# A list-scheduled attention and expert kernel: transfers planned at 260 GB/s, joins of w_outT in place, a table of whole rows, another order of the last accumulators

## The chip, the cores and the metric

The kernel runs on one core of a Trainium2 chip. The metric is the device time of one execution in microseconds (us). Engines are called TensorE (PE), VectorE (DVE), ScalarE (ACT), GpSimd (POOL) and SyncE (SP); SP issues nearly all transfers, GpSimd those with indices. TensorE's weight loads stand in the profile as an engine of their own, PEld.

## The reference

Three steps follow one another, all in float32 but for two matrices of the second:

```python
scores = scale * np.matmul(q, k.transpose(0, 1, 3, 2)) - np.log(S)   # 4 batches, 12 heads, 448 tokens, 64
x = np.matmul(1.0 / (1.0 + np.exp(-scores)), v)                      # then 1792 tokens x 768
h = x @ w_in                                                        # 768 -> 2048
x = np.where(h > 0, h, np.exp(np.minimum(h, 0)) - 1) @ w_out         # 2048 -> 768
logits = x @ w_gate                                                 # 8 experts
for idx in np.argsort(-logits.flatten()):                           # best pairs first, 224 tokens an expert
    ...
out[mask] = np.maximum(x[mask] @ w1[e], 0) @ w2[e]                   # for each expert: 768 -> 1024 -> 768
```

w_in and w_out are float64 and reach the chip as pairs of 32-bit words.

## The kernel before

**Arithmetic.** A float32 factor is split into a high part in TensorE's faster format (`hcopy`, on ScalarE or VectorE) and the rest (`lsub`, always VectorE). A product takes three matmuls: high by high, high by rest, rest by high.

**Stages.** `attention(b)` works through 24 units of two heads for each of 4 batches; its scores go through ScalarE's sigmoid. `layer1(b)` has 16 pieces `f` of 128 columns of w_in, each of 18 matmuls of 128x448 into one of a ring of accumulator banks; a piece is evacuated by two ScalarE functions and two VectorE SCALAR_TENSOR_TENSOR, then split. The second of these VectorE instructions (`zone<-zone,bank 128x448` in the rows) is the last that reads the bank. `layer2(b)` has 6 rows `d` of 48 matmuls over two pieces of w_out. Layer 1 of a batch is interleaved with the attention of the next.

**Joins.** For batch 0 a piece of w_in (768 KB as float64) or w_out (1 MB) is loaded into one of two arena buffers, and `join` (L450) makes float32 of it: ScalarE copies the upper words scaled (ACTIVATE), VectorE masks and shifts them (TENSOR_SCALAR), takes in the sign and then the lower words (two SCALAR_TENSOR_TENSOR). There are 16 + 12 such pieces. The joined piece is written to a DRAM copy, from which later batches load it; each is then split by `hcopy` and `lsub` in `weights` (L495).

**The product of w_out and w_gate.** `through(k)` (L462), six times in layer 1 of batches 1 and 2, before pieces 3, 8 and 13, loads a block of w_outT as two halves of 1 MB, joins each through a slot of the weight ring, and multiplies them by w_gate. It gives the router's logits of the last batch early.

**Rows.** `rows_out` (L663) transposes each 128 columns of x and writes them to two DRAM tables of 512 and 256 columns. For each of 8 experts (phases) VectorE searches the threshold, `listing` (L886) makes the list of tokens, and GpSimd gathers the rows by index: two tables by two groups of 112 tokens, four instructions a phase. `gathered` transposes them on TensorE; `expert` (L970) runs the two layers, with expert weights that stream in as 64 pieces of 768 KB, and scatters rows to the output.

**What sets the order.** All instructions are recorded first. `Plan.run` (L133) then simulates the engines and writes out each engine's queue: at each step the instruction that can start first, and of those within 0.02 us the one with the lowest priority number. That number is the order of creation less a boost (`plan.first(n)`). Its costs are formulas; a transfer ends after its bytes at an assumed rate plus constants. On the chip each engine then executes its queue strictly in that order, so the formulas decide who stands ahead of whom, and the chip's own durations decide who waits. The lines are:

```python
dma = max(dma, s + 1.1) + op.lat      # L195, in Plan.run
op.end = dma + 1.0
lat=n * size / 360e3                  # L279, in Plan.dma, and in fetch (L949)
```

Almost every row of the profile has line L247, where recorded instructions are issued; operations are told apart by their tiles: `zone`, `zone_r` (work tiles), `arena` (raw words), `bank` and `twin` (accumulators, a twin being two banks).

Of the kernel before, what the change touches and what calls it, by code (L numbers as in the profile page):

```python
# [52 lines left out]
class Plan:  # L53
# [79 lines left out]
    def run(self):  # L133
        clock = {e: 0.0 for e in self.eng}
        dma = 0.0
# [26 lines left out]
        while n < len(self.ops):  # L162
# [31 lines left out]
            if e == "SP":  # L194
                dma = max(dma, s + 1.1) + op.lat  # L195
                op.end = dma + 1.0
# [76 lines left out]
    def dma(self, out, in_):  # L273
        size = mybir.dt.size(out.dtype)
        n = 1
        for d in out.shape:
            n *= d
        self.add([("SP", 0.06, lambda: self.eng["SP"].dma_start(out, in_))], [self.region(in_)], [self.region(out)],
                 lat=n * size / 360e3)  # L279

# [10 lines left out]
def kernel(  # L291
# [43 lines left out]
    DA = 4 * P  # L335
    x2rows = [dram.tile([NT, n], F32, name=f"x2rows{i}") for i, n in enumerate((DA, DM - DA))]

# [124 lines left out]
    def through(k):  # L462
# [3 lines left out]
        for hf in range(2):  # L466
            x = r_raw()
            if wide:
                plan.dma(x, w_outT[k, hf])
                y = x.rearrange("p a b -> p (a b)")[:, :KH * P].rearrange("p (a b) -> p a b", b=P).bitcast(F32)  # L470
                join(y, x, r_wd())
            else:
                y = x.rearrange("p a b -> p (a b)")[:, :KH * P].rearrange("p (a b) -> p a b", b=P).bitcast(F32)
                plan.dma(y, w_outT[k, hf])
            ws.append(y.rearrange("p a b -> p (a b)"))
# [100 lines left out]
    def layer1(b):  # L576
        ws = {}
        for f in range(-2, KF):
# [3 lines left out]
            if f < 0:  # L582
                continue
            if b in (1, 2) and f in (3, 8, 13):
                through((b - 1) * 3 + f // 5)
# [77 lines left out]
    def rows_out(b, d, x2, e):  # L663
        rows, pr = r_rows(), sc()[:, 0] if b < B - 1 else twins[0][:, 0]
        with plan.unit():
            for c in range(C):
                PE.transpose(pr[:CP, c * P:(c + 1) * P], x2[:, c * CP:(c + 1) * CP], ident)
        e.copy(rows, pr[:CP, :C * P].rearrange("p (c x) -> p c x", c=C))
        x, o = x2rows[d // 4], d % 4 * P
        plan.dma(x[b * S:(b + 1) * S, o:o + P].rearrange("(c p) x -> p c x", p=CP), rows)  # L670

# [210 lines left out]
    def indirect(reads, writes, lat=GL, **kw):  # L882
        plan.add([("G", 1.05, lambda: plan.eng["G"].indirect_dma_start(**kw))], [plan.region(x) for x in reads],  # L883
                 [plan.region(x) for x in writes], lat=lat)

    def listing(ph):  # L886
# [27 lines left out]
        xg = [r_xg() for _ in range(NA)]  # L914
        for i, c in enumerate((slice(0, DA), slice(DA, DM))):
            for a in range(NA):
                indirect([x2rows[i], idx], [xg[a][:, c]], GL if ph else GL0, out=xg[a][:, c], out_offset=None,
                         in_=x2rows[i], in_offset=bass.IndirectOffsetOnAxis(ap=idx[:, a:a + 1], axis=0))
# [30 lines left out]
    def fetch(g):  # L949
# [7 lines left out]

        plan.add([("SP", 0.06, go)], [(f"reg{ph}", 0, 1, 0, 1)], [plan.region(x)], lat=P * WB * 4 / 360e3)
        h, l = r_eh(), r_el()
# [10 lines left out]
    def expert(ph):  # L970
# [31 lines left out]
        idx = lists.pop(ph)[0]  # L1002
        for a in range(NA):
            y = r_y()
            for n in range(2):
                if ph == E - 1:
                    for f in range(NB):
                        layer(ys, hH, hL, *ws[f // 2], f, f % 2, [2 * a + n])
                AV_.copy(y[:, n * DH:(n + 1) * DH], ys[2 * a + n][:CP, :DH])
            indirect([idx, y], [], out=out, out_offset=bass.IndirectOffsetOnAxis(ap=idx[:, a:a + 1], axis=0),  # L1010
                     in_=y, in_offset=None)

# [80 lines left out]
```

## Time and profile before

| | us |
|---|---|
| median of 3 runs | 1019.3 |
| the three runs | 1016.2, 1019.3, 1023.8 |
| the profiled execution | 1016.5 |
| its span | 1014.7 |
| TensorE busy | 974.2 (96%) |
| VectorE busy | 743.0 (73%) |
| ScalarE busy | 458.1 (45%) |
| GpSimd busy | 60.5 (6%) |
| transfers on SP's queue | 160.48 MB |

The profile is of one execution. Views cut it in different ways: shares of the whole span, shares of chosen stretches (with the granted TensorE clock as a fraction of full speed), groups of like instructions with count and mean duration, sums of waits by what ended them, and the instructions of an engine in order of time. A bracket such as `[2.40 <-DVE zone L247]` says how long the engine stood idle before the row and what ended that. The share of the whole span is an average over stages with different limits, so stretches and single waits tell more.

### The profile page before, as it was taken

To read this page: it belongs to the slowest core of one execution; us is meant where nothing else is said; L and a number is where in the kernel's file an instruction comes from. 1 tells how busy PE (TensorE), PEld (TensorE's weight loads), DVE (VectorE), ACT (ScalarE), POOL (GpSimd) and SP (SyncE) were. 2 spreads that over 40 slices of the span, in tenths; PEclk is the share of its full clock that TensorE was granted. 3 is DMA by queue.
4 is the path that set the end of the run, shared out by engine and by line. 5 is a ranking of instruction groups with operands and counts; after the bars stand their busy time and mean duration, and the time that the engine had idled before them with its cause. 6 is when DMAs were issued, how large, how long until landed. Compare 5 with 4: busy or idle time off the path is not lost. (4 is left out here: it accounts for less than half of the span.)

```text
span 1014.7 us, 15520 instructions
## 1 busy us (share of the span) xinstructions
PE 974.2 (96%) x6039; PEld 807.4 (80%) x6039; DVE 743.0 (73%) x1321; ACT 458.1 (45%) x638; POOL 60.5 (6%) x56
## 2 busy tenths in 40 slices
PE   8999889999999999898999999999999999999996
PEld 3476666787876698775679898887899999998996
DVE  4789996738895344997444597787899898898761
ACT  6868785526765302766421243133433344244220
POOL 0000000000000000000000000001202212123100
PEclk9999999999999999999999999999999999999999
DMA  6876964943455332543123333364656448357720
GB/s 203 298 253 215 307 240 159 320 155 118 166 207 196 108 107 75 180 170 110 63 81 108 103 107 115 104 207 149 203 197 209 165 156 287 150 173 282 264 63 27
DMA packets 53097, 172.47 MB, mean 170 GB/s; under 512 B 6176, under 2 KB 17184, under 8 KB 49952
## 3 DMA queue, kind: packets, MB, share of 16 engines
q1 hardware_dynamic: 49696, 160.48, 47.0%
q0 software_dynamic: 3328, 11.01, 3.5%
q8 instruction: 47, 0.77, 0.3%
q14 instruction: 26, 0.21, 0.1%
HBM read 147.87 MB, written 23.59 MB: 169 GB/s over the span
## 5 line engine op out<-in xcount | busy, mean ns | idle before, releaser
L247 PE MATMUL bank<-zone_r 128*128 128x448 f32 (+1 forms) x3384 | 630.1, 341 | 16.0 <-DVE zone L247 16.0
L247 PEld LDWEIGHTS bank<-zone_r 128*128 128x128 f32 x3384 | 553.6, 190 | 80.5 <-DVE zone L247 19.1
L247 DVE TENSOR_TENSOR zone_r<-zone,zone_r 128x768 fp32r<-128x768 f32 (+3 forms) x347 | 314.1, 917 | 30.5 <-ACT zone_r L247 24.3
L247 PE MATMUL twin<-zone_r 128*112 128x384 f32 (+2 forms) x1416 | 227.0, 355 | 6.8 <-ACT zone L247 5.4
L247 PEld LDWEIGHTS twin<-zone_r 128*112 128x112 f32 (+2 forms) x1416 | 185.3, 175 | 40.1 <-ACT zone L247 17.5
L247 ACT ACTIVATE zone_r<-zone 128x768 fp32r<-128x768 f32 (+3 forms) x192 | 151.0, 800 | 134.0 <-PE bank L247 61.6
L247 DVE CAST zone_r<-zone 128x768 fp32r<-128x768 f32 (+3 forms) x155 | 84.9, 551 | 124.4 <-PE bank L247 96.6
L247 ACT ACTIVATE zone<-bank 128x448 f32<-128x448 f32 x156 | 79.3, 540 | 180.7 <-PE bank L247 168.4
L247 ACT ACTIVATE zone<-twin,bias_s 112x896 f32<-112x896 f32 x96 | 92.8, 1005 | 48.1 <-PE twin L247 47.7
L247 PE MATMUL bank<-zone 112*64 112x448 f32 x384 | 83.6, 553 | 0.9 <-DVE zone_r L247 0.9
L247 ACT ACTIVATE zone_r<-bank 128x448 fp32r<-128x448 f32 x65 | 34.8, 543 | 101.0 <-PE bank L247 100.7
L247 DVE SCALAR_TENSOR_TENSOR zone<-arena,zone 128x1024 int32<-128x1024 int32 (+1 forms) x68 | 74.3, 1094 | 0.7
L883 POOL DMA_INDIRECT zone<-x2rows,idx x32 | 38.8, 1211 | 336.4 <-DVE full L247 214.0
L247 PEld LDWEIGHTS bank<-zone 112*64 112x64 f32 x384 | 22.9, 136 | 37.6 <-issue 35.1
L247 ACT ACTIVATE zone<-arena 128x1024 f32<-128x1024 f32 (+1 forms) x40 | 41.9, 1052 | 22.4 <-DVE zone_r L247 14.6
L247 DVE TENSOR_TENSOR arena<-m,arena 128x896 bf16<-128x896 f32 (+1 forms) x35 | 51.1, 1459 | 0.0
L247 ACT ACT_TABLE_LOAD x35 | 44.9, 1283 | 1.3 <-PEq L1080 0.7
L247 DVE SCALAR_TENSOR_TENSOR zone<-zone 128x448 f32<-128x448 f32 x64 | 39.5, 618 | 4.3 <-ACT zone L247 4.3
L247 ACT ACTIVATE zone<-twin 112x384 f32<-112x384 f32 (+1 forms) x48 | 24.8, 542 | 35.6 <-PE twin L247 24.3
L247 DVE SCALAR_TENSOR_TENSOR zone<-zone,bank 128x448 f32<-128x448 f32 x64 | 39.5, 617 | 1.2
L247 DVE TENSOR_TENSOR zone_r<-bank,zone_r 128x448 fp32r<-128x448 f32 x45 | 27.5, 617 | 11.1 <-ACT zone_r L247 9.3
L247 DVE TENSOR_SCALAR zone<-zone 128x1024 int32<-128x1024 int32 (+1 forms) x40 | 25.4, 636 | 13.8 <-ACT zone L247 13.7
(105 smaller groups left out, 310.2 us busy)
## 6 DMA issues: line engine op xcount, KB each, us to landing
zone<-we SPq DMA_DIRECT2D x64, 768.0 KB, 5.7
zone<-wcopy SPq DMA_DIRECT2D x48, 384.0 KB, 3.1
zone<-wcopy SPq DMA_DIRECT2D x36, 512.0 KB, 3.3
arena<-w_in SPq DMA_DIRECT2D x16, 768.0 KB, 5.1
arena<-w_out SPq DMA_DIRECT2D x12, 1024.0 KB, 6.0
arena<-w_outT SPq DMA_DIRECT2D x12, 1024.0 KB, 5.8
zone<-kq SPq DMA_DIRECT2D x23, 448.0 KB, 3.4
wcopy<-zone SPq DMA_DIRECT2D x16, 384.0 KB, 4.1
```

The source lines that it names most:

```text
L247: fn = lambda: getattr(self.eng[e], name)(*args, **kw)
L883: plan.add([("G", 1.05, lambda: plan.eng["G"].indirect_dma_start(**kw))], [plan.region(x) for x in reads], [plan.region(x) for x in writes ...
```

## The change

It has five parts. The planner takes transfers at 260 GB/s instead of 360 and one constant as 1.0 instead of 1.1 us, which makes the whole order anew. `through` stands before pieces 1, 6 and 11; its loads and joins get a priority number 300 higher, and the join works in place in the arena, with shifts and masks on every second word: four VectorE instructions a half instead of three, and no slot of the weight ring. A third DRAM table holds whole rows of 768 columns; `rows_out` writes each tile to it as well (24 writes more), and all phases but the first gather from it with two instructions instead of four. The loop over the output halves of an expert is turned, so that the last expert's four accumulators are filled in the order 0, 2, 1, 3, and its last copy is shared by ScalarE and VectorE.

```diff
@@ -192,7 +192,7 @@
             clock[e] = s + c
             op.end = s + c + op.lat
             if e == "SP":
-                dma = max(dma, s + 1.1) + op.lat
+                dma = max(dma, s + 1.0) + op.lat
                 op.end = dma + 1.0
             [a for a in op.alts if a[0] == e][0][2]()
             for o in op.succs:
@@ -276,7 +276,7 @@
         for d in out.shape:
             n *= d
         self.add([("SP", 0.06, lambda: self.eng["SP"].dma_start(out, in_))], [self.region(in_)], [self.region(out)],
-                 lat=n * size / 360e3)
+                 lat=n * size / 260e3)
 
 
 class Engine:
@@ -333,7 +333,7 @@
     psum = ctx.enter_context(tc.tile_pool(name="psum", bufs=1, space=PSUM))
     dram = ctx.enter_context(tc.tile_pool(name="dram", bufs=1, space=bass.MemoryType.DRAM))
     DA = 4 * P
-    x2rows = [dram.tile([NT, n], F32, name=f"x2rows{i}") for i, n in enumerate((DA, DM - DA))]
+    x2rows = [dram.tile([NT, n], F32, name=f"x2rows{i}") for i, n in enumerate((DA, DM - DA, DM))]
 
     class Ring:
         def __init__(self, tiles):
@@ -466,9 +466,17 @@
         for hf in range(2):
             x = r_raw()
             if wide:
-                plan.dma(x, w_outT[k, hf])
-                y = x.rearrange("p a b -> p (a b)")[:, :KH * P].rearrange("p (a b) -> p a b", b=P).bitcast(F32)
-                join(y, x, r_wd())
+                y = x.rearrange("p a b -> p (a b)")[:, :KH * P].rearrange("p (a b) -> p a b", b=P)
+                lo, hi = (x.rearrange("p c (f two) -> p c f two", two=2)[:, :, :, i] for i in range(2))
+                with plan.first(-300):
+                    plan.dma(x, w_outT[k, hf])
+                    V.tensor_scalar(lo, lo, 29, None, op0=ALU.logical_shift_right)
+                    V.scalar_tensor_tensor(out=lo, in0=hi, scalar=-0x80000000, in1=lo, op0=ALU.bitwise_and,
+                                           op1=ALU.bitwise_or)
+                    A.activation(f32(hi), f32(hi), AF.Copy, scale=2.0 ** -112)
+                    V.tensor_scalar(hi, hi, 0x0FFFFFFF, 3, op0=ALU.bitwise_and, op1=ALU.logical_shift_left)
+                    V.tensor_tensor(out=y, in0=hi, in1=lo, op=ALU.bitwise_or)
+                y = f32(y)
             else:
                 y = x.rearrange("p a b -> p (a b)")[:, :KH * P].rearrange("p (a b) -> p a b", b=P).bitcast(F32)
                 plan.dma(y, w_outT[k, hf])
@@ -581,7 +589,7 @@
                     ws[f + 2] = weights(b, f + 2)
             if f < 0:
                 continue
-            if b in (1, 2) and f in (3, 8, 13):
+            if b in (1, 2) and f in (1, 6, 11):
                 through((b - 1) * 3 + f // 5)
             h, l = ws.pop(f)
             ps = mm()
@@ -666,8 +674,8 @@
             for c in range(C):
                 PE.transpose(pr[:CP, c * P:(c + 1) * P], x2[:, c * CP:(c + 1) * CP], ident)
         e.copy(rows, pr[:CP, :C * P].rearrange("p (c x) -> p c x", c=C))
-        x, o = x2rows[d // 4], d % 4 * P
-        plan.dma(x[b * S:(b + 1) * S, o:o + P].rearrange("(c p) x -> p c x", p=CP), rows)
+        for x, o in ((x2rows[d // 4], d % 4 * P), (x2rows[2], d * P)):
+            plan.dma(x[b * S:(b + 1) * S, o:o + P].rearrange("(c p) x -> p c x", p=CP), rows)
 
     load_pair(0)
     load_pair(1)
@@ -912,7 +920,7 @@
         V.tensor_scalar(hi_[:CP, :NA], l2[:, :, 0], 8.0, None, op0=ALU.mult)
         V.tensor_tensor(out=idx, in0=hi_[:CP, :NA], in1=l2[:, :, 1], op=ALU.add)
         xg = [r_xg() for _ in range(NA)]
-        for i, c in enumerate((slice(0, DA), slice(DA, DM))):
+        for i, c in ((2, slice(0, DM)),) if ph else ((0, slice(0, DA)), (1, slice(DA, DM))):
             for a in range(NA):
                 indirect([x2rows[i], idx], [xg[a][:, c]], GL if ph else GL0, out=xg[a][:, c], out_offset=None,
                          in_=x2rows[i], in_offset=bass.IndirectOffsetOnAxis(ap=idx[:, a:a + 1], axis=0))
@@ -955,7 +963,7 @@
         def go():
             SP.dma_start(x, we[ds(regs[ph], 1), i, :, 0, :].rearrange("o p f -> (o p) f"))
 
-        plan.add([("SP", 0.06, go)], [(f"reg{ph}", 0, 1, 0, 1)], [plan.region(x)], lat=P * WB * 4 / 360e3)
+        plan.add([("SP", 0.06, go)], [(f"reg{ph}", 0, 1, 0, 1)], [plan.region(x)], lat=P * WB * 4 / 260e3)
         h, l = r_eh(), r_el()
         for p in range(2):
             c = slice(p * WB // 2, (p + 1) * WB // 2)
@@ -1000,15 +1008,20 @@
             for t in range(2):
                 layer(ys, hH, hL, wh, wl, 2 * i + t, t, range(2 * NA))
         idx = lists.pop(ph)[0]
-        for a in range(NA):
-            y = r_y()
-            for n in range(2):
+        y = [r_y() for _ in range(NA)]
+        for n in range(2):
+            for a in range(NA):
+                k = 2 * a + n
+                c0, last = n * DH, ph == E - 1 and (a, n) == (NA - 1, 1)
                 if ph == E - 1:
                     for f in range(NB):
-                        layer(ys, hH, hL, *ws[f // 2], f, f % 2, [2 * a + n])
-                AV_.copy(y[:, n * DH:(n + 1) * DH], ys[2 * a + n][:CP, :DH])
-            indirect([idx, y], [], out=out, out_offset=bass.IndirectOffsetOnAxis(ap=idx[:, a:a + 1], axis=0),
-                     in_=y, in_offset=None)
+                        layer(ys, hH, hL, *ws[f // 2], f, f % 2, [k])
+                for i, e in enumerate((A, V) if last else (AV_,)):
+                    w = DH // 2 if last else DH
+                    e.copy(y[a][:, c0 + i * w:c0 + (i + 1) * w], ys[k][:CP, i * w:(i + 1) * w])
+                if n:
+                    indirect([idx, y[a]], [], out=out, in_=y[a], in_offset=None,
+                             out_offset=bass.IndirectOffsetOnAxis(ap=idx[:, a:a + 1], axis=0))
 
     def products(g0, i, cs, ps, xg, opened=False):
```

Counts: VectorE has 1335 instructions instead of 1321, ScalarE 602 instead of 603, GpSimd's queue 14 gathers less, SP 322 issues instead of 298; TensorE has the same matmuls.

The order of VectorE's queue in layer 1 of batch 0, before: between the evacuation of piece 12 and that of piece 14 (`zone<-zone,bank` rows are evacuations; TENSOR_SCALAR and `zone<-arena` rows of 128x1024 are joins of w_out, of 128x768 those of w_in; TENSOR_TENSOR are splits).

```order
L247 TENSOR_SCALAR zone<-zone 128x1024
L247 TENSOR_TENSOR zone_r<-zone,zone_r 128x448
L247 SCALAR_TENSOR_TENSOR zone<-arena_77,zone 128x1024 x2
L247 SCALAR_TENSOR_TENSOR zone<-zone 128x448
L247 TENSOR_TENSOR zone_r<-zone,zone_r 128x1024
L247 SCALAR_TENSOR_TENSOR zone<-zone,bank_70 128x448
L247 SCALAR_TENSOR_TENSOR zone<-zone 128x448
L247 TENSOR_SCALAR zone<-zone 128x1024
L247 TENSOR_TENSOR zone_r<-zone,zone_r 128x448
L247 SCALAR_TENSOR_TENSOR zone<-arena_76,zone 128x1024
L247 SCALAR_TENSOR_TENSOR zone<-zone,bank_71 128x448
```

The same place in the changed order, up to the evacuation of piece 14:

```order
L247 TENSOR_TENSOR zone_r<-zone,zone_r 128x896
L247 TENSOR_TENSOR zone_r<-zone,zone_r 128x768
L247 TENSOR_SCALAR zone<-zone 128x1024
L247 SCALAR_TENSOR_TENSOR zone<-zone,bank_71 128x448
L247 SCALAR_TENSOR_TENSOR zone<-arena_77,zone 128x1024
L247 TENSOR_TENSOR zone_r<-zone,zone_r 128x448
L247 SCALAR_TENSOR_TENSOR zone<-arena_77,zone 128x1024
L247 SCALAR_TENSOR_TENSOR zone<-zone 128x448
L247 CAST zone_r<-zone 128x1024
L247 SCALAR_TENSOR_TENSOR zone<-zone,bank_72 128x448
```

Before, the fourth and fifth pieces of w_out are joined here; in the changed order it is the first, and the evacuations of pieces 13 and 14 have four pieces less of w_out ahead of them.

The end of TensorE's queue, before (the last matmuls of the last expert; `twin0` and `twin1` of the program print as twin_73 and twin_74, and a wait for VectorE is printed as DVE with the number of a semaphore):

```order
L247 MATMUL twin_73<-zone_r 112x384 x6
L247 MATMUL twin_73<-zone_r 112x384 [waits DVE_49]
L247 MATMUL twin_73<-zone_r 112x384 x20
L247 MATMUL twin_74<-zone_r 112x384 x27
L247 MATMUL twin_74<-zone_r 112x384 [waits DVE_49]
L247 MATMUL twin_74<-zone_r 112x384 x20
```

And in the changed order, where the two double banks print as twin_74 and twin_75:

```order
L247 MATMUL twin_74<-zone_r 112x384 x3
L247 MATMUL twin_75<-zone_r 112x384 x24
L247 MATMUL twin_74<-zone_r 112x384 [waits DVE_49]
L247 MATMUL twin_74<-zone_r 112x384 x23
L247 MATMUL twin_75<-zone_r 112x384 [waits DVE_49]
L247 MATMUL twin_75<-zone_r 112x384 x23
```

Before, the second half of each twin follows its first half and waits there for a copy; in the changed order 24 matmuls of the other twin lie between.

GpSimd's queue for the second and third expert, before (`zone<-x2rows` is a gather, `out<-zone` a scatter; the number behind x2rows is the table):

```order
L883 DMA zone<-x2rows_65,idx_120 112x512 x2
L883 DMA zone<-x2rows_66,idx_120 112x256 x2
L883 DMA out<-zone,idx_119 1792x768 x2
L883 DMA zone<-x2rows_65,idx_121 112x512 x2
L883 DMA zone<-x2rows_66,idx_121 112x256 x2
L883 DMA out<-zone,idx_120 1792x768 x2
```

And in the changed order:

```order
L891 DMA zone<-x2rows_67,idx_121 112x768 x2
L891 DMA out<-zone,idx_120 1792x768 x2
L891 DMA zone<-x2rows_67,idx_122 112x768 x2
L891 DMA out<-zone,idx_121 1792x768 x2
```

Two gathers of 112x768 stand where four of 112x512 and 112x256 stood; the scatters keep their places.

## Rows read from the trace of the kernel before

**Rows 1.** The page's busy times: us, share of the span, instructions.
```profile
PE 974.2 (96%) x6039; PEld 807.4 (80%) x6039; DVE 743.0 (73%) x1321; ACT 458.1 (45%) x638; POOL 60.5 (6%) x56
```
**Rows 2.** Stretches: us, busy us of PE, PEld, DVE, ACT, POOL, clock, DMA, GB/s.
```profile
57.00:146.00 89.00, 77.27 (x388) 60.19 (x386) 83.53 (x116) 74.85 (x102) 0.00 (x0) 0.98 0.72 246
146.00:225.00 79.00, 78.80 (x420) 60.97 (x421) 48.71 (x57) 34.99 (x43) 0.00 (x0) 1.00 0.67 225
225.00:400.00 175.00, 173.84 (x925) 135.84 (x924) 113.56 (x166) 81.01 (x108) 0.00 (x0) 1.00 0.44 144
400.00:475.00 75.00, 67.72 (x358) 50.82 (x356) 67.21 (x111) 54.02 (x72) 0.62 (x3) 0.98 0.45 156
```
**Rows 3.** Waits of PE by releaser: us in total, times, longest.
```profile
PE bank L247 <- DVE zone L247: 17.2, 13, 3.0
```
**Rows 4.** PE in order of time, 110 to 147 us: start, us, instruction, idle before.
```profile
111.60 1.48 PE L247 MATMUL twin<-zone_r 64*112 64x448 f32 x12
113.01 1.72 PE L247 MATMUL bank<-zone 112*64 112x448 f32 x8
117.16 12.93 PE L247 MATMUL bank<-zone_r 128*128 128x448 f32 x54 [2.43 <-DVE zone L247]
...
138.61 5.19 PE L247 MATMUL bank<-zone_r 128*128 128x448 f32 x24 [0.28 <-DVE zone L247]
146.20 1.08 PE L247 MATMUL bank<-zone_r 128*128 128x448 f32 x4 [2.40 <-DVE zone L247]
```
**Rows 5.** Groups of DVE instructions by form: count, busy us, mean ns, idle before.
```profile
L247 DVE TENSOR_TENSOR zone_r<-zone,zone_r 128x1024 fp32r<-128x1024 f32 x48 | 58.6, 1221 | 11.7 <-ACT zone_r L247 10.0
...
L247 DVE SCALAR_TENSOR_TENSOR zone<-arena,zone 128x1024 int32<-128x1024 int32 x36 | 43.8, 1220 | 0.3
...
L247 DVE TENSOR_TENSOR zone_r<-zone,zone_r 128x896 fp32r<-128x896 f32 x23 | 25.0, 1087 | 0.4
L247 DVE CAST zone_r<-zone 128x1024 fp32r<-128x1024 f32 x35 | 24.3, 693 | 62.6 <-PE bank L247 62.4
...
L247 DVE TENSOR_SCALAR zone<-zone 128x1024 int32<-128x1024 int32 x24 | 16.5, 689 | 4.3 <-ACT zone L247 4.3
L247 DVE CAST zone_r<-zone 128x448 fp32r<-128x448 f32 x41 | 16.1, 393 | 3.5 <-ACT zone L247 1.8
...
L247 DVE CAST zone_r<-zone 128x896 fp32r<-128x896 f32 x16 | 10.0, 624 | 18.6 <-PE twin L247 12.4 <-DMA zone<-kq 3.5 <-DMA arena<-w_out 2.7
```
**Rows 6.** Transfers by issue: count, KB each, median us from issue to landing.
```profile
arena<-w_in SPq DMA_DIRECT2D x16, 768.0 KB, 5.1
arena<-w_out SPq DMA_DIRECT2D x12, 1024.0 KB, 6.0
```
**Rows 7.** Groups of ACT and of POOL instructions by form, as in rows 5.
```profile
L247 ACT ACTIVATE zone<-arena 128x1024 f32<-128x1024 f32 x24 | 27.3, 1146 | 16.9 <-DVE zone_r L247 13.4 <-DMA arena<-w_outT 2.3 <-DMA arena<-w_out 1.1
L883 POOL DMA_INDIRECT zone<-x2rows,idx x32 | 38.8, 1211 | 336.4 <-DVE full L247 214.0 <-DVE arena L247 58.9 <-DMA x2rows<-zone 21.7
```
**Rows 8.** The two stretches of 25 us with a lower granted clock, as in rows 2.
```profile
100.00:125.00 25.00, 21.18 (x99) 17.07 (x99) 23.55 (x33) 19.16 (x28) 0.00 (x0) 0.93 0.86 286
450.00:475.00 25.00, 20.50 (x110) 13.12 (x108) 20.83 (x43) 18.33 (x23) 0.62 (x3) 0.93 0.37 121
```
**Rows 9.** DVE in order of time, 34 to 47 us, one row.
```profile
36.90 0.56 DVE L247 TENSOR_SCALAR zone<-zone 128x768 int32<-128x768 int32 x1 [2.59 <-ACT zone L247]
```
**Rows 10.** PE in order of time, single waits from 456 us to the end.
```profile
460.88 5.47 PE L247 MATMUL bank<-zone_r 128*128 128x448 f32 x18 [2.96 <-DVE zone L247]
...
692.49 1.04 PE L247 MATMUL twin<-ident,zone 112*128 112x112 f32 x8 [1.69 <-DMA zone<-x2rows,idx]
...
934.91 0.41 PE L247 MATMUL bank<-ident,zone 112*128 112x112 f32 x2 [1.41 <-DMA zone<-x2rows,idx]
...
994.44 8.63 PE L247 MATMUL twin<-zone_r 128*112 128x384 f32 x48 [0.65 <-DVE zone L247]
1003.72 3.94 PE L247 MATMUL twin<-zone_r 128*112 128x384 f32 x21 [0.65 <-DVE zone L247]
```

## Prediction

> **What bounds the kernel now.** I read the busy shares first, then the stretches, then what TensorE waits for, and then single waits in order of time. TensorE is busy 974.2 us, 96% of the span [rows 1], and the change gives it the same 6039 matmuls, so no order of the work can go below that; the profiled execution takes 1016.5 us, and only its idle time and its slow clock can be won. The stretches show where that lies [rows 2]. From 57 to 146 us (layer 1 of batch 0, with the float64 words joined on VectorE) TensorE works 77.27 of 89.00 us and VectorE 83.53: there VectorE is the bound. From 400 to 475 it is the same in small, 67.72 of 75.00 us against 67.21. From 146 to 400 TensorE is nearly full, and VectorE has 79.00 - 48.71 = 30.3 us to spare in the first of those stretches. The list of waits agrees: of TensorE's idle time 17.2 us, in 13 waits, stands against VectorE results in the accumulator banks [rows 3]. The reader is to see that a transfer is seldom what TensorE waits for. What the assumed rate of transfers changes is which VectorE instruction the planner puts ahead of which.
>
> **Batch 0, layer 1.** TensorE stood 2.43 us at 117.16 and 2.40 us at 146.20 for VectorE [rows 4]. At 146.20 it waited for the evacuation of the last of the 16 pieces. In the order of before, VectorE has ahead of that evacuation joins of w_out that the changed order puts behind it: four TENSOR_SCALAR of 128x1024 at 0.689 us, six SCALAR_TENSOR_TENSOR at 1.220 us and two splits (TENSOR_TENSOR) at 1.221 us [rows 5], 2.76 + 7.32 + 2.44 = 12.5 us. Four pieces of attention work (three of about 0.62 us, the row of a CAST of 128x896, and a split of 128x896 at 1.087) move behind it too, 2.95 us, and five copies that ScalarE had move ahead of it: two CASTs of 128x896 at 0.624, two of 128x448 at 0.393, one of 128x1024 at 0.693 [rows 5], 2.73 us. That is 12.5 + 2.95 - 2.73 = 12.7 us less. But the evacuation is also wanted earlier: one attention unit (1.48 + 1.72 = 3.2 us, overlapping to 3.1) and 24 matmuls of layer 2 (5.19 us, of it 4.9 before the next can start) [rows 4] stood ahead of it on TensorE and now come after: 8.0 us. The wait shrinks by 12.7 - 8.0: **-4.7 us**. Bounds: 0, if VectorE is only idle longer in the first 57 us, and -8, if all the waits of VectorE on this stretch go. The 12.5 us of joins aren't gone: the 30.3 us spare VectorE time of the next stretch hides them. If that were filled, they would come back as waits in layer 2 one for one.
>
> **Loads just in time.** The planner believes that a piece of w_in (786,432 bytes) takes 786/260 + 2.0 = 5.0 us instead of 786/360 + 2.1 = 4.3, and one of w_out (1,048,576) 6.0 instead of 5.0; the medians in the trace are 5.1 and 6.0 [rows 6]. So its new belief is near what this kernel sees. Between two joins in the same arena buffer the changed order leaves on average 8.4 us of VectorE work (6.6 to 10.1, against 4.7 to 5.9 in before). A load (6.0) and ScalarE's copy (1.146 [rows 7]) want 7.2. I cost this at nothing; the margin of 1.2 us is the cover.
>
> **The clock.** The granted clock is 1.00 in nearly all stretches and 0.93 in two of 25 us [rows 8]: 3.5 us at 1.2 GHz and the rest at 2.4, which costs half of 3.5, 1.75 us, each time. Both began after TensorE had idled, 2.43 us at 117.16 [rows 4] and 2.96 us at 460.88 [rows 10]. Both idles should shrink. I count one dip as gone, **-1.75 us** (bounds 0 and -3.5).
>
> **Joins of w_outT (batches 1 and 2).** Each of 12 halves has four VectorE instructions for three: a shift and a mask of one source, and two of two sources. The two-source ones cost 1.220 as they do now. The others read and write every second word in place, which no row of before does; they lie between 0.689 (the same operation, contiguous) and 1.220 (the two-source one on the same strided arena) [rows 5]. I take 0.689, the row of the same operation: 0.69 + 1.22 + 0.69 + 1.22 = 3.82 us against 3.13, 0.69 x 12 = 8.3 us more VectorE work in all. At 1.22 it is 4.88, 21 us more. In batch 1 (225 to 400 us) TensorE is at 173.84 of 175.00 and VectorE has 61 us to spare [rows 2], and the halves stand with lowest priority behind everything that is ready: **+0.3 us** (bounds 0 and +6).
>
> The Trainium skill, page "VectorE: DVE Perf Modes", section "What auto-detection actually checks", gives the double rate to a single-source operation within SBUF whose outermost dimension is even, and names no stride for it; by that rule 0.69 holds and the sum is the one here. Its paragraph on the plain mode, on the same page, lists odd strides among what falls back to it; by that, the first rival below holds. No run of before shows which.
>
> In batch 2 (400 to 475 us) the wait of 2.96 us at 460.88 [rows 10] is again for VectorE. There I added up, for each matmul that waits, VectorE's work ahead of the result it wants less TensorE's own work ahead. The growth of this difference over the stretch is what must be waited: 6.1 us in before, 4.8 after, **-1.3 us** (bounds -6 and +2, the latter with 1.22 a shift).
>
> **Gathers.** From the second expert on, 2 gathers of whole rows replace 4 at 1.211 us each on GpSimd [rows 7]. If a gather of 768 columns costs the same, the rows are asked for 2.4 us earlier; if it costs by its bytes (1.5 times the mean), 1.2 us. Of the four waits for rows the 1.41 us at 934.91 and 0.5 of another then go. The 1.69 us at 692.49 [rows 10] is the first expert, whose gathers stay; its transposes stand some 5 us of work later on TensorE, so it goes too. Against this: each row tile is written to two tables, 24 more writes of 224 KB, and a row buffer is held until both have landed; +0.9 us on the first gather that waits for rows. Together **-2.7 us** (bounds -5 and +1).
>
> **The end.** The accumulators of the last expert share two double banks. Before, the second half of a pair starts when VectorE has copied the first out of the same double bank: 0.65 us at 994.44 and again at 1003.72 [rows 10]. In the new order the other double bank is worked on between, 24 matmuls or some 4 us, against 0.65 to hide: -1.3 us. The last copy of 384 columns in two halves on two engines: -0.2. **-1.5 us** (bounds -1.8 and 0).
>
> **Sum:** -4.7 - 1.75 + 0.3 - 1.3 - 2.7 - 1.5 = -11.65, so 1016.5 becomes 1004.9. The median of before is 1019.3, 2.8 above its profiled execution; I add that and get 1007.7, **1008 us**.
>
> **Rivals.**
> 1. *The strided shifts run at one element a cycle.* 24 instructions x 0.53 = 12.7 us more VectorE work. In batch 1 about +6 comes through, in batch 2 the -1.3 turns into +2 and the dip there stays (1.75). 1008 + 5.7 + 3.3 = 1017; with the dip at nearly 1019: no change. For it: strided in place is in no row. Against: the stretch of batch 1 has 61 us of spare VectorE time.
> 2. *Loads come too late, slower.* ScalarE is busy 74.85 of 89.00 us from 57 to 146 [rows 2], so its copy may stand 2 us in its queue: 6.0 + 1.15 + 2 = 9.2 us against 8.4 between two joins in one buffer. VectorE then idles 0.8 to 0.9 us at each of 26 pieces (28 less the first two), 22 us, while it is the bound: 1008 + 22 = 1030, slower. It decides from a chain above 8.4 us on. For it: VectorE already waits 2.59 us for such a copy at 36.90 [rows 9]. Against: the new order spaces joins wider than the old, and the old lost little that way.
> 3. *The gain of layer 1 is given back.* Attention of batch 1 moves some 18 us of TensorE work later; if its evacuations pile up on VectorE as the joins did, only gathers and end remain: 1019.3 - 4.2 = 1015. For it: what moves behind a stall is still to be done by the same engine. Against: the 30.3 us spare after 146 us.
>
> **Chances.** Forecast 0.50, its own range 1001 to 1014. Rival 1 0.15, rival 2 0.13, rival 3 0.22. A measurement tells about 1% from no change: below 1009.1 is faster, above 1029.5 slower. Faster: 0.44 of the forecast's 0.50 and 0.02 of the rivals' edges, 0.46. Slower: 0.08 of rival 2 and 0.02 of a rival 1 with worse knock-on, 0.10. The rest, 0.44, is no change. The range 997 to 1021 leaves out rival 2 and the forecast's best end, about 0.17.
>
> **What would show it.** Right: from 57 to 146 us TensorE's idle time falls from 11.7 to about 7; the waits on VectorE in the banks fall from 17.2 to about 11; one of the two 0.93 stretches is 1.00; strided TENSOR_SCALAR rows of 128x1024 at about 0.69; the waits of 0.65 at the end are gone; waits for gathered rows near 2. Wrong: strided rows near 1.2 (rival 1); VectorE idle before joins with ScalarE or the arena load named (rival 2); TensorE's idle time moved to 146 to 225 us (rival 3).

## The result and the profile after

| | us |
|---|---|
| kernel before, median of 4 runs | 1017.8 |
| changed kernel, median of 4 runs (1005.3 to 1010.6) | 1007.1 |
| ratio | 0.9891, 95% interval 0.9852 to 0.9930 |
| changed kernel again (e9), median of 6 runs | 1010.0 beside 1019.0 |
| ratio in e9 | 0.9920, 95% interval 0.9899 to 0.9940 |
| the profiled execution, its span | 1010.6, 1008.8 |

The change makes the kernel about 1% faster: 10.6 us by the first comparison, 9.0 by the second. The profiled execution is the slowest of its four, so the profile shows less than the medians: a span 5.9 us shorter than that of before.

The page of the changed kernel, busy times as in [rows 1]:

```profile
PE 976.4 (97%) x6039; PEld 811.5 (80%) x6039; DVE 752.6 (75%) x1335; ACT 445.8 (44%) x631; POOL 45.6 (5%) x42
```

TensorE is busy 2.2 us longer than before, with the same matmuls, and more of its time passed at the lower clock (below). All of the gain is idle time, which falls by 8.1 us. The stretches, as in [rows 2], with two of the expert stage added:

```profile
57.00:146.00 89.00, 83.52 (x424) 64.56 (x423) 80.48 (x115) 70.52 (x96) 0.00 (x0) 0.98 0.68 232
146.00:225.00 79.00, 79.00 (x421) 62.26 (x420) 58.83 (x68) 40.31 (x50) 0.00 (x0) 1.00 0.75 257
...
225.00:400.00 175.00, 171.47 (x908) 132.24 (x908) 118.24 (x172) 78.54 (x109) 0.00 (x0) 0.99 0.50 164
...
400.00:475.00 75.00, 71.09 (x371) 57.23 (x371) 65.63 (x111) 48.95 (x70) 0.61 (x3) 1.00 0.41 139
680.00:720.00 40.00, 36.00 (x272) 32.80 (x271) 28.34 (x69) 13.89 (x22) 3.73 (x4) 0.91 0.49 154
720.00:940.00 220.00, 215.78 (x1782) 205.69 (x1779) 196.18 (x460) 83.59 (x131) 32.38 (x23) 0.99 0.58 203
```

Idle time is the length of a stretch less PE's busy time. From 57 to 146 us it falls from 11.73 to 5.48, from 400 to 475 from 7.28 to 3.91; from 225 to 400 it rises from 1.16 to 3.53. VectorE works 10.1 us more than before from 146 to 225 us: the joins that moved behind, in time that was spare. Cutting the first stretch at 118 us shows the place more sharply. Before:

```profile
57.00:118.00 61.00, 53.04 (x275) 40.38 (x274) 56.99 (x82) 51.73 (x71) 0.00 (x0) 1.00 0.73 248
118.00:147.00 29.00, 25.04 (x119) 20.56 (x118) 27.53 (x36) 24.12 (x33) 0.00 (x0) 0.95 0.72 245
```

After:

```profile
57.00:118.00 61.00, 59.83 (x305) 48.03 (x304) 58.78 (x89) 50.67 (x74) 0.00 (x0) 1.00 0.64 215
118.00:147.00 29.00, 24.69 (x126) 17.46 (x125) 22.70 (x28) 20.35 (x24) 0.00 (x0) 0.94 0.77 272
```

Of 7.96 us of idle time before 118 us, 1.17 are left; behind it 3.96 have become 4.31. The gain lies where w_in is joined, not where w_out is.

TensorE's waits, as in [rows 3]:

```profile
PE bank L247 <- DVE zone L247: 10.1, 5, 2.8
PE twin L247 <- DMA zone<-x2rows,idx: 3.3, 2, 2.7
```

Thirteen waits for VectorE are five, 17.2 us are 10.1. TensorE in order of time, as in [rows 4, 10]:

```profile
128.39 1.90 PE L247 MATMUL bank<-zone_r 128*128 128x448 f32 x5 [2.68 <-DVE zone L247]
...
250.51 2.00 PE L247 MATMUL bank<-zone_r 128*128 128x448 f32 x7 [2.38 <-DVE zone L247]
...
417.39 1.86 PE L247 MATMUL bank<-zone_r 128*128 128x448 f32 x8 [2.85 <-DVE zone L247]
...
709.95 0.64 PE L247 MATMUL twin<-ident,zone 112*128 112x112 f32 x2 [2.67 <-DMA zone<-x2rows,idx]
...
985.27 16.92 PE L247 MATMUL twin<-zone_r 128*112 128x384 f32 x96
```

The first row is the wait for the evacuation of the last piece, which [rows 4] show at 146.20. It now ends 17.8 us earlier, but TensorE still waits 2.68 us. The row at 250.51 is new, in batch 1. The last one is the end: 96 matmuls without a wait between them.

### The profile page after: what moved, and what is told of

The parts are those of the page before. It is cut to its first block, busy times and chain, and to the rows that moved or that the text cites. A ratio compares the mean times of both kernels' runs of the same rounds, so it can differ in the third digit from the quotient of the medians.

```text
span 1008.8 us, 15529 instructions
## 1 busy us (share of the span) xinstructions
PE 976.4 (97%) x6039; PEld 811.5 (80%) x6039; DVE 752.6 (75%) x1335; ACT 445.8 (44%) x631; POOL 45.6 (5%) x42
## 5 line engine op out<-in xcount | busy, mean ns | idle before, releaser
L247 PE MATMUL bank<-zone_r 128*128 128x448 f32 (+1 forms) x3384 | 633.7, 343 | 12.9 <-DVE zone L247 10.1
L247 DVE SCALAR_TENSOR_TENSOR zone<-arena,zone 128x768 int32<-128x768 int32 (+1 forms) x56 | 59.8, 1068 | 1.0
L247 ACT ACTIVATE zone<-twin 112x384 f32<-112x384 f32 (+2 forms) x48 | 24.7, 536 | 50.3 <-DVE zone L247 20.0
L891 POOL DMA_INDIRECT zone<-x2rows,idx x18 | 24.2, 1343 | 340.6 <-PE bank L247 234.8
L247 DVE CAST zone_r<-bank 128x448 fp32r<-128x448 f32 x13 | 8.1, 623 | 36.1 <-PE bank L247 36.1
L247 ACT ACTIVATE zone<-arena 128x768 f32<-128x768 f32 (+1 forms) x28 | 28.1, 1004 | 2.2 <-DMA arena<-w_out 1.3
```

The source lines that it names most:

```text
L247: fn = lambda: getattr(self.eng[e], name)(*args, **kw)
```

## The experiments

TensorE's idle time, worked out from the stretches of each run's profile as above, in us:

| kernel | 57-118 | 118-147 | 225-400 | 400-475 | 680-720 | 720-940 | ratio to before |
|---|---|---|---|---|---|---|---|
| before | 7.96 | 3.96 | 1.16 | 7.28 | 3.36 | 3.81 | 1 |
| changed kernel | 1.17 | 4.31 | 3.53 | 3.91 | 4.00 | 4.22 | 0.9891 |
| e1, new rate alone | 1.33 | 4.32 | 4.28 | 5.84 | 1.98 | 8.01 | 1.0007 |
| e2, the other parts, old rate | 7.48 | 4.03 | 1.62 | 1.88 | 2.39 | 1.87 | 0.9950 |
| e3, float64 loads at 260 alone | 1.53 | 5.25 | 1.87 | 5.87 | 3.45 | 4.04 | 0.9914 |
| e4, changed, joins of before | 1.22 | 2.79 | 1.35 | 5.56 | 4.25 | 4.22 | 0.9906 |
| e5, changed, no third table | 1.34 | 4.33 | 3.19 | 3.36 | 1.78 | 7.27 | 0.9893 |
| e7, changed, only float64 loads at 260 | 1.74 | 4.68 | 5.71 | 1.72 | 4.32 | 1.88 | 0.9898 |
| e8, gate on w_out | 8.45 | 4.32 | 1.65 | 6.07 | 3.57 | 4.05 | 0.9999 |
| e11, w_in at 260 alone | 1.84 | 7.64 | 2.24 | 5.79 | 3.35 | 3.52 | 0.9941 |
| e12, w_out and w_outT at 260 alone | 5.61 | 5.04 | 2.51 | 6.06 | 3.27 | 2.96 | 1.0012 |

**e1: the new rate alone.**

```diff
-dma = max(dma, s + 1.1) + op.lat
+dma = max(dma, s + 1.0) + op.lat
-lat=n * size / 360e3
+lat=n * size / 260e3
```

> The kernel before with the new transfer rate and constant alone. Theory A (the rate puts joins of w_out behind the evacuations of layer 1 of batch 0): TensorE's idle time from 57 to 146 us falls from 11.7 to 5 to 7 us, the copies at the end still cost 1.3 us, the time falls by 5 to 8 us. Theory B (the gain comes from the four other parts, the rate only shuffles): within 2 us of before.

Measured: 1018.6 us, ratio 1.0007 (0.9986 to 1.0028). By the time it is Theory B, by the profile Theory A: the idle time from 57 to 118 us goes as in the changed kernel, 6.6 us. What it wins there it loses elsewhere, 3.1 us from 225 to 400, 4.2 from 720 to 940, and in the clock: 17.1 us of this profile ran at 1.2 GHz, against 6.8 of before, which is at most 5.1 us of work. This is not one profile alone: the mean granted clock of its 12 runs is 0.990, that of the 23 runs of before beside it 0.994, which over the span is an estimated 3.8 us more. The expert stage, in the view of stretches:

```profile
720.00:940.00 220.00, 211.99 (x1708) 201.30 (x1707) 188.94 (x446) 77.60 (x120) 46.74 (x33) 0.97 0.53 190
```

and in its list of TensorE's waits, the ones for gathered rows:

```profile
PE bank L247 <- DMA zone<-x2rows,idx: 4.4, 3, 2.0
```

**e2: the other four parts at the old rate.**

```diff
-lat=n * size / 260e3
+lat=n * size / 360e3
-dma = max(dma, s + 1.0) + op.lat
+dma = max(dma, s + 1.1) + op.lat
```

> The changed kernel with the old rate and constant. Theory A: TensorE's idle time from 57 to 146 us stays at 10 us or more, only the end (-1.5 us) and part of the waits in batch 2 go: 2 to 5 us less than before. Theory B: 8 to 11 us less, as the whole change.

Measured: 1010.6 us, ratio 0.9950 (0.9923 to 0.9977). By the stretches it is Theory A: the idle time from 57 to 147 us stays at 11.5 us, and 5.4 of 7.3 us go in batch 2, 2.9 in the expert stage. Outside the table 3.8 us come in from 147 to 225 us, where before had none. The time, 5 to 6.5 us less, lies between the ranges of the two theories.

**e3: only the loads of float64 words at 260.** The edit is to the kernel before:

```diff
-lat=n * size / 360e3)
+lat=n * size / (260e3 if n * size >= 786432 else 360e3))
```

> The kernel before, where the planner takes only the loads of float64 words (w_in, w_out, w_outT, 768 KB and more) at 260 GB/s, all others at 360 and with the old constant. Theory A: this alone brings the idle time from 57 to 146 us down to 5 to 7 us and the time by 4 to 7 us. Theory B, or a gain that comes from the other transfers' rate: within 2 us of before.

Measured: 1007.8 us, ratio 0.9914 (0.9884 to 0.9944): 28 loads of batch 0 and 12 of w_outT, planned near their real length, bring about as much as the whole change, and more than the 4 to 7 us of Theory A. The expert stage is left as it was in before.

**e4 and e5: one part taken out of the changed kernel.** e4 puts the joins of w_outT and their places back, e5 leaves out the third table:

```diff
-if b in (1, 2) and f in (1, 6, 11):
+if b in (1, 2) and f in (3, 8, 13):
...
-with plan.first(-300):
-    plan.dma(x, w_outT[k, hf])
...
+plan.dma(x, w_outT[k, hf])
+join(y, x, r_wd())
```

> The changed kernel with the joins of w_outT of before (through at 3, 8, 13, normal priority, out of place). Theory A (batch 0 is worth some 6 us, the joins of w_outT 3): TensorE's idle time before 225 us stays near 10 us, from 400 to 475 us it rises from 3.9 to 5.5 or more, and the time is 1 to 4 us above the changed kernel's 1007. Rival C (the new joins in place cost what they bring, since the changed kernel idles 3.5 us from 225 to 300 us where before idled 1.0): within 1 us of 1007 or below it.

```diff
-for i, c in ((2, slice(0, DM)),) if ph else ((0, slice(0, DA)), (1, slice(DA, DM))):
+for i, c in ((0, slice(0, DA)), (1, slice(DA, DM))):
...
-for x, o in ((x2rows[d // 4], d % 4 * P), (x2rows[2], d * P)):
+for x, o in ((x2rows[d // 4], d % 4 * P),):
```

> The changed kernel without the third table: four gathers a phase again and each row tile written once. Theory A (the gathers are what the rate alone had lost in the expert stage): the waits for gathered rows rise from 3.3 to 6 us or more, and the time is 3 to 6 us above 1007, near that of the rate alone at the layers' gain. Rival D (the expert stage's losses with the rate alone were a chance of that order): within 2 us of 1007.

Measured: 1009.3 us (0.9906, 0.9873 to 0.9940) and 1009.5 us (0.9893, 0.9861 to 0.9925). Neither can be told from the changed kernel (0.9891, and 0.9920 in e9) by its time. The stretches say more. With the joins of before the idle time of batch 1 is 1.35 instead of 3.53, that of batch 2 5.56 instead of 3.91: the new joins cost in one batch what they bring in the other. Without the table the idle time from 720 to 940 us is 7.27 instead of 4.22, and that from 680 to 720, where the first expert waits for its rows, 1.78 instead of 4.00. All waits for rows are 4.5 us against 3.3, not 6 or more. Theory A's prices (1 to 4 us, 3 to 6 us) did not come in the time.

**e6: zero matmuls where TensorE waits for the first expert's rows.** All queues stay as they are; in `gathered`:

```diff
+for _ in range(0 if ph else 12):
+    plan.group.append((0.0, lambda: plan.eng["PE"].matmul(ps[:, :S], idle[:, :P], idle[:, :S], ...
 for a in range(NA):
+    for _ in range(16 if a and not ph else 0):
+        plan.group.append((0.0, lambda: plan.eng["PE"].matmul(ps[:, S:512], idle[:, :P], idle[:, S:512], ...
```

> The changed kernel with 28 matmuls of zeros on TensorE in front of the transposes that wait for the first expert's last rows (3.3 us of idle time at 706 to 710 us), all queues as they were. Theory E (TensorE's idle time is followed by 3.4 or 6.8 us at the lower clock): the stretch at the lower clock that begins at 709 us is gone, 3 us less than 1007. Rival: the clock falls there all the same, and the time stays within 1 us.

Measured: 1006.6 us, ratio 0.9881 (0.9838 to 0.9924); against the changed kernel's 0.9891 and 0.9920 the expected 3 us can't be told from nothing. In its profile the clock of the stretch is 1.00, where the changed kernel has 0.91 (PE's busy time contains the zero matmuls):

```profile
680.00:720.00 40.00, 39.31 (x326) 35.61 (x325) 31.55 (x77) 17.51 (x26) 3.73 (x4) 1.00 0.61 196
```

**e7: the changed kernel, float64 loads alone at 260.** It has the line of e3 in the changed kernel, and 360 and 1.1 for all else.

> The changed kernel in which only the loads of float64 words are taken at 260 GB/s, all others at 360 and with the constant of before. Theory A: as the other transfers' rate does not matter, within 2 us of 1007. If the gains of the raw loads' rate alone (-9 us on the kernel before) and of the four other parts at the old rate (-5 us) add up: near 1003.

Measured: 1007.5 us, ratio 0.9898 (0.9850 to 0.9945). The time is the changed kernel's, and the gains do not add up. Together with the others it separates two causes in the stretch from 720 to 940 us. Without the table TensorE idles 3.0 to 4.1 us in the five kernels where the expert weights are planned at 360 (before, e3, e8, e11, e12), 8.01 and 7.27 where at 260 (e1, e5); with the table 1.87 and 1.88 at 360 (e2, e7), 4.22 at 260. So the lower rate costs 2 to 5 us there. The table brings 3.05 at 260 (e5 against the changed kernel, the one pair that differs in the table alone), and at 360 some 1 to 2, together with the other parts. e7 loses its gain of 2.3 us again from 225 to 400 us, where it idles 5.71 instead of 3.53. Its expert stage:

```profile
720.00:940.00 220.00, 218.12 (x1826) 209.44 (x1826) 197.85 (x460) 89.70 (x137) 29.30 (x23) 1.00 0.60 209
```

**e8: fewer joins of w_out ahead of the last evacuations, at the old rate.**

```diff
-with plan.first(3000):
+with plan.first(3000), plan.after(gL[:, 13, :]) if b == 0 and i == 2 else nullcontext():
     ws[i] = weights(b, KF + i)
```

> The kernel before, rate 360 and all, with one more dependency: the third piece of w_out is loaded only once the 14th piece of layer 1 of batch 0 is split, so three pieces of w_out instead of five and a half are joined ahead of the last evacuation. Theory A (the joins ahead of the evacuations are what costs, whatever the rate): the waits of 2.4, 1.3 and 2.4 us between 114 and 147 us shrink by 3 us or more together, TensorE's idle time from 57 to 146 us falls to 8 or 9 us. Rival F (the rate helps by something else, such as loads that no longer collide): the idle time stays above 11 us.

Measured: 1017.3 us, ratio 0.9999 (0.9979 to 1.0018). It is a miss for the step that the prediction rests on. The last evacuation comes 9 us earlier, and TensorE reaches it 11 us earlier, since the planner draws its matmuls forward as well. The two waits of 1.29 and 2.40 become one of 4.32, in TensorE's order of time:

```profile
137.07 6.66 PE L247 MATMUL bank<-zone_r 128*128 128x448 f32 x24 [4.32 <-DVE zone L247]
```

**e9 and e10: the changed kernel again, and a mix.** The mix has the joins of before in batch 1 (before pieces 3, 8 and 13), the new ones in batch 2 (1, 6 and 11), and the zero matmuls of e6.

> The changed kernel itself, beside the others on one chip: 1005 to 1010 us by every theory.

> The changed kernel with the joins of before in batch 1, the new ones in batch 2, and the zero matmuls in front of the transposes of the first expert. Theory A with the clock's: TensorE's idle time from 225 to 300 us falls from 3.5 to 1 us, the stretch at the lower clock at 250 us goes with it, and the one at 709 us: 3 to 6 us below the changed kernel beside it. Rival (each new order brings its own waits elsewhere): within 2 us of it.

Measured on one chip: 1010.0 us (0.9920, 0.9899 to 0.9940) and 1007.0 us (0.9885, 0.9861 to 0.9909). The intervals overlap a little; five of six runs of the mix lie below the lowest of the changed kernel. The idle time from 225 to 400 us is 0.57 instead of 3.60, and the stretch at the lower clock there is gone. The mix is 3.0 us below the changed kernel; as it has both edits, the 3.0 us can't be given to either. With e6 (0.9881) it is the fastest version tried.

**e11 and e12: w_in or w_out alone.** The kernel before, with the condition of e3 as `n * size == 786432` (the 16 loads of w_in) and as `n * size >= 1048576` (w_out and w_outT).

> The kernel before, where the planner takes only the 16 loads of w_in at 260 GB/s. Theory G (the gain of layer 1 of batch 0 lies in its first two thirds, where the joins of w_in stand ahead of the evacuations): TensorE's five waits of 1.0 to 2.4 us between 57 and 118 us, 7.8 together, fall to 3 or less; those from 118 to 147 us stay at 3 or more. Theory A as in the prediction (it lies in the joins of w_out ahead of the last evacuations): the five waits stay.

> The kernel before, where the planner takes only the 24 loads of w_out and w_outT at 260 GB/s. Theory G: the five waits between 57 and 118 us stay at 7 us or more together, and the time is above that of the run with w_in. Theory A as in the prediction: the waits at 131 and 146 us, 3.7 together, go by 3 us or more, and the time falls by 3 us or more.

Measured: 1012.2 us (0.9941, 0.9920 to 0.9962) and 1019.4 us (1.0012, 0.9993 to 1.0031). The stretches of e11, and then of e12:

```profile
57.00:118.00 61.00, 59.16 (x300) 49.43 (x299) 59.39 (x88) 49.65 (x74) 0.00 (x0) 1.00 0.67 225
118.00:147.00 29.00, 21.36 (x112) 13.32 (x112) 27.06 (x33) 21.23 (x25) 0.00 (x0) 0.82 0.80 278
```

```profile
57.00:118.00 61.00, 55.39 (x288) 42.63 (x288) 56.88 (x83) 51.23 (x72) 0.00 (x0) 1.00 0.73 246
118.00:147.00 29.00, 23.96 (x105) 18.94 (x105) 26.97 (x36) 24.75 (x32) 0.00 (x0) 0.88 0.68 239
```

Theory G: the 16 loads of w_in alone take 6.1 of the 6.8 us. With w_out still planned too short, one wait of 7.64 us follows at 122 us, with 10.2 us at the lower clock, and the run wins 0.6% all the same. w_out alone takes away 2.4 us before 118, gives 1.1 back behind it, and moves nothing in the time. With both (e3) the longest wait there is one of 4.20 us.

## Why the prediction was right, and where it was not

The time (1008 against 1007.1), the sign and the size (-11.65 against -10.6 and -9.0) were right. That the number is so close is partly luck: the terms were worked out for the profiled execution, whose span fell by 5.9 us and not by 11.65, and the six as the profiles show them add up to less still, -2.2 us with the clock at its full 5.1. Of the six terms of the sum one stands nearly as it was worked out, three had the right sign and another size, and two the wrong sign. The largest term was right in its mechanism, VectorE joins ahead of evacuations, but named the wrong joins.

- **Batch 0, layer 1: -4.7 predicted, -6.2 in the profile (idle time from 57 to 146 us), in another place.** The step "VectorE has ahead of that evacuation joins of w_out that the changed order puts behind it" described the order truly, but not the gain: the wait for that evacuation is 2.68 us instead of 2.40, and e8, which begins three joins of w_out ahead of it instead of six, wins nothing. (In e12 five of the six still begin ahead of it, so e12 does not test this step.) The gain is in the waits between 57 and 118 us, and e11 shows that it hangs on the 16 loads of w_in.

  The order of VectorE's queue shows how. Here are the first and the eighth evacuation, before:

```profile
66.85 0.62 DVE L247 SCALAR_TENSOR_TENSOR zone<-zone,bank 128x448 f32<-128x448 f32 x1
...
101.76 0.61 DVE L247 SCALAR_TENSOR_TENSOR zone<-zone,bank 128x448 f32<-128x448 f32 x1
```

  And after:

```profile
57.07 0.61 DVE L247 SCALAR_TENSOR_TENSOR zone<-zone,bank 128x448 f32<-128x448 f32 x1
...
81.41 0.62 DVE L247 SCALAR_TENSOR_TENSOR zone<-zone,bank 128x448 f32<-128x448 f32 x1
```

  A join of w_in begins on VectorE with a mask (TENSOR_SCALAR of 128x768). Before, 8 of the 16 masks stand in the queue ahead of the first evacuation and 15 ahead of the eighth; in the changed kernel 6 and 10. All kernels measured fall into two groups. Where 8 and 15 stand there (before, e2, e8, e12), TensorE idles 5.6 to 8.5 us from 57 to 118 us; where 6 and 10 or 12 do (all others), 1.2 to 1.8. The planner that believes the words of w_in land earlier puts more of their joins ahead of the evacuations. This is read from the queues; a kernel in which only these places are exchanged was not run.

  I counted VectorE's work ahead of the last evacuation and took its idle time before that as unchanged. It was not: by 118 us VectorE has worked 97.3 us instead of 92.9 (35.91 and 38.55 us up to 57, and the rows above). But the gain does not rest on that idle time. The masks' waits for ScalarE's copies are, before, after and in e3:

```profile
L247 DVE TENSOR_SCALAR zone<-zone 128x768 int32<-128x768 int32 x16 | 8.9, 557 | 9.5 <-ACT zone L247 9.4
```

```profile
L247 DVE TENSOR_SCALAR zone<-zone 128x768 int32<-128x768 int32 x16 | 8.9, 554 | 6.7 <-ACT zone L247 6.4
```

```profile
L247 DVE TENSOR_SCALAR zone<-zone 128x768 int32<-128x768 int32 x16 | 8.9, 554 | 13.2 <-ACT zone L247 13.2
```

  They fall by 2.8 us in the changed kernel, stay at 9.4 in e11 and rise to 13.2 in e3, and all three win 6 us or more of TensorE's idle time between 57 and 118 us.

- **Loads just in time: 0 predicted, and rival 2 (slower) did not happen.** Loads of w_in land in 4.7 us and of w_out in 5.9, against 5.0 and 6.0 believed. Rival 2 named waits that exist, those of the masks above, but they were in before already, and the change shortened them.

```profile
arena<-w_in SPq DMA_DIRECT2D x16, 768.0 KB, 4.7
arena<-w_out SPq DMA_DIRECT2D x12, 1024.0 KB, 5.9
```

- **The clock: -1.75 predicted, +5.1 in the profile.** The wrong sign. Before had two stretches at half speed:

```profile
117.50:120.90 3.40, 3.40 (x11) 3.05 (x10) 3.36 (x6) 1.88 (x5) 0.00 (x0) 0.50 1.02 324
462.20:465.60 3.40, 3.40 (x11) 3.01 (x10) 3.13 (x4) 2.45 (x3) 0.00 (x0) 0.50 0.65 230
```

  The changed kernel has four, 17.0 us together:

```profile
128.80:132.20 3.40, 3.40 (x11) 3.04 (x10) 3.31 (x5) 3.37 (x5) 0.00 (x0) 0.50 1.02 346
251.70:255.10 3.40, 3.40 (x11) 3.05 (x10) 2.72 (x4) 3.04 (x4) 0.00 (x0) 0.50 0.16 64
709.10:715.90 6.80, 5.95 (x28) 5.95 (x29) 3.49 (x6) 0.54 (x1) 0.10 (x1) 0.50 0.28 92
896.80:900.20 3.40, 3.40 (x24) 3.33 (x23) 3.06 (x6) 0.00 (x0) 0.22 (x1) 0.50 0.28 95
```

  This is at most (17.0 - 6.8) / 2 = 5.1 us of work. TensorE's busy time rose by 2.2 us only, and that is what parts the 8.1 us by which the idle time fell from the 5.9 of the span; where the rest of the 5.1 went is not shown. Over six runs (e9) the mean granted clock is 0.990, beside 0.993 in 17 runs of before, an estimated 3.5 us of the time. All four stretches begin in a wait or within 1.5 us of the end of one, as in before. The step that failed is "both idles should shrink": one of them did not, and new ones came.

- **Joins of w_outT, batch 1: +0.3 predicted, +2.4 of idle time.** The duration was right. The shifts and masks on every second word take 689 ns, as the contiguous ones did, so rival 1 is out. The Trainium skill, page "VectorE: DVE Perf Modes", section "What auto-detection actually checks", names no stride among the conditions of this double rate, and the trace agrees.

```profile
L247 DVE TENSOR_SCALAR arena<-arena 128x1024 int32<-128x1024 int32 x24 | 16.3, 689 | 1.1 <-ACT arena L247 0.7 <-DMA arena<-w_outT 0.3
```

  The cover failed: the 61 us that VectorE has to spare from 225 to 400 us lie mostly behind 300. Up to there it works 68.03 of 75 us, and 67.26 in before already, and TensorE waits 1.15 and 2.38 us for evacuations. e4 takes the new joins out and has 1.35 us of idle time instead of 3.53. The joins are not all that decides this stretch, though: e1 has the joins of before too and idles 4.28 us there.

- **Joins of w_outT, batch 2: -1.3 predicted, -3.4 (and -2.4 in e9).** The right sign, mis-sized. A part of it is not the joins': e8, whose edit is in batch 0, idles 6.07 us there instead of 7.28, and putting the joins of before back into the changed kernel (e4) costs 1.65. The kernels with the new joins idle 1.7 to 4.9 us there, those with the joins of before 5.6 to 7.3.

- **Gathers: -2.7 predicted, +1.0 (680 to 940 us).** The two late waits went as worked out: all waits for rows now lie in the first expert, 3.3 us instead of 5.0. But the 1.69 us there did not go; 2.67 us stand in its place, and other waits came between 720 and 940. What the term left out is that the new rate itself costs 2 to 5 us there (e1, e5 against the kernels without the table at 360; e2, e7 against the changed kernel). The table alone is worth 3.05 us from 720 to 940 us (e5), near what the term expected, but e5 wins 2.2 us back from 680 to 720, and nothing of it is seen in the time.

- **The end: -1.5 predicted, -1.1.** Both waits of 0.65 us are gone, 1.3 us. The copy in two halves was to bring 0.2 and costs 0.16: ScalarE's half begins 0.39 us behind VectorE's, and from the last matmul's end to the last scatter's issue it is 1.03 us instead of 0.87.

- **Rival 3 (given back)** is what happened to the rate alone (e1), though not by attention piling up after 146 us, where TensorE is full: it was given back in batch 1, in the expert stage and to the clock.

What stays open is why the lower rate of the other transfers makes TensorE wait longer in the expert stage, though the 64 expert weights land in 5.7 us, believed to be 5.0 at 260 and 4.3 at 360. It is open too which order would have the gains of all stages: e2, e3 and the changed kernel each have gains that the others lack, and e7 shows that they don't add up.

## What to carry to other kernels

Where a planner writes the order out, a wrong cost harms at the few instructions that wait for it: planning 16 transfers near the length that the trace shows was worth 0.6% here, planning all transfers at that rate nothing. Change such a constant for one class of instructions at a time, and judge it by each stage's idle time, since the sum hides gains and losses of the same size. Spare time of an engine, averaged over a long stretch, is no cover for work that falls into its busy part.

## What was not expected of the hardware

TensorE's clock fell to 1.2 GHz for 3.4, 6.8 or 10.2 us beside waits of about 1 to 8 us, and not at each long one: the wait of 2.85 us at 417.39 was followed by none in one profile of the changed kernel, and one of 3.07 us at the same place by 3.4 us in the other (e9). Matmuls of zeros in place of a wait took one such stretch away (e6, 709 us), though not visibly in the time. Profiles of kernels of one percent's difference had between 6.8 and 20.5 us at the lower clock, up to 7 us of work, so a gain of a few microseconds of idle time can be covered by it.
